# One transfer instead of two halves for the first K block of a cached-attention kernel

## The chip, the cores and the metric

The kernel runs on one core of a Trainium2 chip. The metric is device time in microseconds (us) of one execution. Three runs of the kernel before the change took 1298.83, 1298.94 and 1298.96 us, so the median is 1298.94 us.

A core has a matrix engine (TensorE, "PE" in the rows, with its weight loads as "PEld"), a vector engine (VectorE, "DVE"), a scalar engine (ScalarE, "ACT"), GpSimd ("POOL") and a sync engine (SyncE, "SP") which here only issues DMA transfers. Transfers run on 16 DMA engines. On-chip memory has 128 partitions; a "row" of a transfer below is what one partition receives.

## The reference

The computation is one decoding step: layer norm of x, attention of one query against a long cache, a small MLP as a gate, and a residual. Sizes: 2 batches, 32 heads, 8192 cached keys per head, 128 elements per key, all in 32-bit floats.

```python
def _A_ref(x, k_cache, v_cache, wq, wo):
    q = (x @ wq).reshape(B, Sq, H, Dh).transpose(0, 2, 1, 3)
    scores = jnp.einsum("bhqd,bhkd->bhqk", q, k_cache) * (Dh ** -0.5)
    p = _softmax(scores, axis=-1)
    o = jnp.einsum("bhqk,bhkd->bhqd", p, v_cache)
    return o.transpose(0, 2, 1, 3).reshape(B, Sq, H * Dh) @ wo

def _B_ref(x, w1, b1, w2, b2):
    h = _gelu(jnp.einsum("bsd,df->bsf", _layernorm(x), w1) + b1)
    return jnp.einsum("bsf,fd->bsd", h, w2) + b2

xn = _layernorm(x)
return x + _A_ref(xn, k_cache, v_cache, wq, wo) * _silu(_B_ref(xn, w1, b1, w2, b2))
```

The caches are nearly all of the data: K and V hold 268 MB each.

## The kernel before

The 64 combinations of batch and head are worked off as N = 32 pairs. The K of a pair is a block of 128 partitions by 64 KB (128 keys of 128 floats on each partition, 8.39 MB), and so is its V. There are three such buffers: `kb[0]` and `kb[1]` take the K blocks in turn (pair n goes to `kb[(n+1) % 2]`, so pair 0 goes to `kb[1]`), and `vb` takes the V blocks. Before the pairs, `kb[0]` holds the query weights wq and `vb` the MLP weights and the start's small tensors.

For a pair n the work is:

- `scores_mul` (L555, DVE, once for each half s of the block, 64 keys per partition each): multiply K by the query, in place.
- `scores_sum` (L562, DVE, once for each half): sum over the 128 elements, which gives the scores.
- `max_rows` (L566 on DVE, L569 on PE) and `max_dve` (L572, DVE): the maximum, which crosses partitions by a transpose on PE.
- `exps` (L578 on PE, L579 to L587 on ACT): the exponentials, PZ.
- `weighted` (L606 on PE, 64 matmuls): probabilities times V.
- `spread` (L621, DVE): the result put in its place for the final projection.

The loop over pairs is software-pipelined by hand. While DVE works on the scores of pair n, it also does the maximum of pair n-1, between the two multiplications of pair n, and after it ACT and PE do the exponentials and the weighted sum of pair n-1. Pair 0 and pair 31 stand outside a hardware loop; pairs 1 to 30 are 15 turns of a loop with two pairs in each turn.

All loads are issued by SP, in program order, on one DMA queue, by the helper `load` at L329. The order is: w1, x, w2, b1, b2, wq, K of pair 0, K of pair 1, V of pair 0, K of pair 2, V of pair 1, and so on to K of pair 31, V of pair 30, V of pair 31 (into `kb[1]`), and the pieces of the output weights wo (into `vb`). Below, k0, k1, ... and v0, v1, ... stand for these K and V transfers. SP waits before a load until its buffer is free: k1 for the query matmuls L513 that read wq, v0 for the last reader of the start's tensors, k(n+2) for the scores of pair n (the row is that of L566), v(n) for the matmuls L606 of pair n-1.

Three kinds of blocks come as two transfers of 32 KB a row: K of pair 0, K of pair 31 and V of pair 31. All others are one transfer of 64 KB a row. Each kind of transfer has a semaphore of its own on which its readers wait: the halves of k0 have k10 and k11, the whole blocks of `kb[0]` and `kb[1]` have kb0 and kb1.

A planner (`Plan`) records all operations, works out from the tiles read and written which semaphore values each must wait for, and writes them out in program order; it moves nothing. Inside the hardware loop a wait's value is a multiple of the turn, plus a constant where that is needed; a constant costs a register instruction.

Of the kernel before, what the change touches and what calls it, by code (L numbers as in the profile page):

```python
# [164 lines left out]
def decode_kernel(nc, x, kc, vc, wq, wo, w1, b1, w2, b2, out):  # L165
# [9 lines left out]
    N = B * HH  # L175
# [152 lines left out]
    def load(dst, src, sem, w, over=()):  # L328
        op("sp", lambda: nc.sync.dma_start(dst, src), (), w, over=over, dma=sem)  # L329

    def load_k(n):
        i = (n + 1) % 2
        if n in (0, N - 1):
            for s in range(2):
                load(kbuf[i][:, s * M:(s + 1) * M], kf[n][:, s * M:(s + 1) * M], f"k{i}{s}", [("kb", i, s)])
            return
        load(kbuf[i], kf[n], f"kb{i}", [("kb", i, s) for s in range(2)])
# [10 lines left out]
    for t, src, k in ((b1_sb, b1, "b1"), (b2_sb, b2, "b2")):  # L348
        load(t.rearrange("o (k e) -> o k e", k=16), src.rearrange("(o k e) -> o k e", o=1, k=16), k, [k])
    load(wq_sb, wq.rearrange("(p c) n -> p c n", p=P), "wq", [("kb", 0, s) for s in range(2)])  # L350
    load_k(0)


# [177 lines left out]

    PT, PM, PN = (t for t in scratch[:3])
    load_k(1)

    def load_v(n):
# [90 lines left out]
    for n in range(N):  # L626
        scores_mul(n, 0)
        if n:
            max_dve(n - 1)
            exps(n - 1)  # L630
        scores_mul(n, 1)

        if n:
            weighted(n - 1)
            if n < N - 1:
                load_v(n)
        scores_sum(n, 0)
        scores_sum(n, 1)
        max_rows(n)
        if n:  # L640
            spread(n - 1)

        if n + 2 < N:
            load_k(n + 2)
        elif n + 2 == N:
            for s in range(2):
                load(kbuf[1][:, s * M:(s + 1) * M], vf[N - 1][:, s * M:(s + 1) * M], f"v1{s}", [("kb", 1, s)])
# [104 lines left out]
```

## Time and profile before

The profiled execution took 1298.91 us; its span, from the first to the last instruction, is 1297.6 us, so 1.31 us lie around it. It is 0.03 us below the median of the runs.

| | profile before |
|---|---|
| time of the profiled execution | 1298.91 us |
| span | 1297.6 us |
| DVE busy | 1138.0 us, 88% of the span |
| PE busy | 407.6 us, 31% |
| data moved by DMA | 559.42 MB, 431 GB/s mean |
| first multiplication of pair 0 on DVE starts | 52.27 us |
| last piece of wo used from | 1293.51 us |

In the rows of the profile, a line of a timeline gives start, length, engine, source line, operation, output and input, count, and in brackets the idle time before it with what ended that. A line of a window gives the window, then busy time and count on each engine, the clock granted to TensorE, the DMA engines' busy share and the GB/s that landed in the window. "DMA to landing" is the time from the issue on SP to the transfer's completion, as least, median and greatest of the transfers in the lines above it.

### The profile page before, as it was taken

Reading aid. Unit: us, or ns where it says so; the run is one execution under the profiler, and the core shown is the slowest. Engines: PE = TensorE matmul, PEld = TensorE weight load, DVE = VectorE, ACT = ScalarE, POOL = GpSimd, SP = SyncE. Lnnn points to the kernel's source line nnn. Section 1 sums busy time; section 2 is a strip of 40 time slices with the busy share of each in tenths; the row PEclk is TensorE's granted clock in tenths of the full one; section 3 lists DMA queues with packets and bytes.
Section 4 is the critical chain, followed back from the end, with each engine's and each line's share of the span. In section 5 each row is a group of like instructions: output and inputs, shape, how many; then the busy total and the mean of one; then the engine's idle time right before and its main releaser. Section 6 shows DMA issues by size and latency. Waiting matters only on the chain.

```text
span 1297.6 us, 6944 instructions
## 1 busy us (share of the span) xinstructions
PE 407.6 (31%) x2796; PEld 123.4 (10%) x2796; DVE 1138.0 (88%) x294; ACT 78.0 (6%) x250; POOL 1.4 (0%) x8
## 2 busy tenths in 40 slices
PE   5703333312333312333311333321333321233328
PEld 1100110000101000101100101100001100001103
DVE  3599999988889988889988888988888988888991
ACT  1200000000000000000000000000000000000000
POOL 0000000000000000000000000000000000000000
PEclk9856666556666656666656666656666655666658
DMA  9999999999999999999999999999999999999998
GB/s 404 445 425 440 428 432 438 426 444 424 434 438 424 446 424 440 430 426 444 426 438 430 430 440 426 444 424 434 438 424 446 424 432 438 424 446 426 425 433 372
DMA packets 11231, 559.42 MB, mean 431 GB/s; under 512 B 1364, under 2 KB 1620, under 8 KB 1880
## 3 DMA queue, kind: packets, MB, share of 16 engines
q1 hardware_dynamic: 11224, 559.33, 99.7%
q8 instruction: 4, 0.07, 0.0%
q14 instruction: 3, 0.02, 0.0%
HBM read 559.30 MB, written 0.03 MB: 431 GB/s over the span
## 4 chain that ended last, share of the span: by engine, by line
DMA 71%; PE 24%; DVE 3%; issue 1%; ACT 0%; SPq 0%; DVEq 0%
DMA vb<-in_A_v_cache_dram 68%; PE po L606 22%; DMA vb<-in_A_wo_dram 2%; DVE kb L555 1%; DVE sc L562 1%; PE s L433 1%; DMA vb<-in_A_x_dram 1%; PE po L513 1%; PE s L479 0%; PE s L435 0%; DVE vb L441 0%; DVE vb L380 0%; ACT L454 0%; PE acc L696 0%; PE s L486 0%
## 5 line engine op out<-in xcount | busy, mean ns | idle before, releaser
L555 DVE TENSOR_TENSOR kb<-kb,Q 128x8192 f32<-128x8192 f32 x64 | 555.5, 8681 | 99.6 <-DMA kb<-in_A_k_cache_dram 93.1
L562 DVE TENSOR_REDUCE sc<-kb 128x64 f32<-128x8192 f32 x64 | 552.3, 8666 | 0.0
L606 PE MATMUL po<-vb,PZ 128*8 128x512 f32 x1984 | 282.3, 733 | 286.1 <-DMA vb<-in_A_v_cache_dram 284.8
L578 PE MATMUL s<-nm,srow 1*128 1x2 f32 x64 | 18.6, 358 | 360.8 <-DVE nm L572 360.8
L606 PEld LDWEIGHTS po<-vb,PZ 128*8 128x8 f32 x1984 | 56.3, 103 | 485.9 <-issue 482.4
L569 PE MATMUL s<-ident,mx 128*1 128x128 f32 x32 | 11.8, 369 | 197.8 <-DVE mx L566 197.8
L578 PEld LDWEIGHTS s<-nm,srow 1*128 1x128 f32 x64 | 15.9, 306 | 370.1 <-DVE nm L572 370.1
L613 ACT COPY o<-po 128x512 f32<-128x512 f32 x32 | 18.8, 586 | 528.2 <-PE po L606 528.2
L579 ACT COPY bias<-s 128x2 f32<-128x2 f32 x32 | 5.1, 160 | 623.9 <-PE s L578 623.9
L615 PE MATMUL s<-mod,o 128*128 128x2 f32 x256 | 33.6, 253 | 22.1 <-ACT o L613 22.1
L615 PEld LDWEIGHTS s<-mod,o 128*128 128x128 f32 x256 | 31.1, 191 | 51.4 <-ACT o L613 51.4
L583 ACT ACTIVATE PZ<-sc,bias 64x128 f32<-64x128 f32 x64 | 25.5, 399 | 1.8
L569 PEld LDWEIGHTS s<-ident,mx 128*1 128x1 f32 x32 | 2.5, 79 | 201.4 <-DVE mx L566 170.8
L621 DVE TENSOR_TENSOR Z<-blk,s 128x8 f32 (+1 forms) x32 | 5.2, 163 | 13.3 <-PE s L615 13.3
L441 DVE COPY vb<-vb 2x384 f32<-2x384 f32 x4 | 1.8, 499 | 15.4 <-ACT vb L437 15.4
L433 PE MATMUL s<-vb 128*2 128x512 f32 (+1 forms) x24 | 12.1, 654 | 0.3 <-ACT vb L393 0.3
L583 ACT ACTIVATION_READ_ACCUMULATOR PZ<-sc,bias 64x1 f32 x64 | 11.8, 185 | 0.0
L566 DVE TENSOR_REDUCE mx<-sc 128x1 f32<-128x128 f32 x32 | 9.2, 286 | 1.1
L587 ACT ACTIVATE ZR<-half,rs 128x8 f32 (+1 forms) x32 | 9.6, 301 | 4.1
L606 PE MATMUL po<-kb,PZ 128*8 128x512 f32 x64 | 9.4, 754 | 1.4 <-ACT PZ L583 1.4
L572 DVE TENSOR_REDUCE nm<-s 1x2 f32<-1x128 f32 x32 | 8.7, 272 | 0.3 <-PE s L569 0.3
L688 DVE COPY wide<-x 128x32 f32<-128x32 f32 x1 | 0.2, 195 | 9.0 <-ACT o L686 9.0
(101 smaller groups left out, 90.3 us busy)
## 6 DMA issues: line engine op xcount, KB each, us to landing
kb<-in_A_k_cache_dram SPq DMA_DIRECT2D x4, 4096.0 KB, 42.9
kb<-in_A_v_cache_dram SPq DMA_DIRECT2D x2, 4096.0 KB, 40.9
vb<-in_B_w_dram SPq DMA_DIRECT2D x2, 2752.0 KB, 12.1
vb<-in_A_wo_dram SPq DMA_DIRECT2D x1, 4096.0 KB, 19.0
vb<-in_A_wo_dram SPq DMA_DIRECT2D x1, 2048.0 KB, 23.6
vb<-in_A_wo_dram SPq DMA_DIRECT2D x1, 1280.0 KB, 26.2
vb<-in_A_wo_dram SPq DMA_DIRECT2D x2, 256.0 KB, 26.3
vb<-in_A_v_cache_dram SPq DMA_DIRECT2D x31, 29.5
```

What stands on the lines that cost most here:

```text
L433: pe(lambda f=f, w=w, ph=ph, c=c: matmul(ph[:B, :w], yT[:, c, :], w1_sb[:, c, f:f + w], start=(c == 0), stop=False), ["yT", "w1"], [k])
L513: pe(lambda i=i, c=c, wv=wv, a=a, j=j, hd=hd: matmul(PO[R * j:R * j + NQ * B, :].rearrange("m (h d) -> m h d", d=DH), xnT[:, c, a:a + NQ * ...
L555: vector(n, n, lambda n: nc.vector.tensor_tensor(out=k, in0=k, in1=cols(Q, n * DH, DH).unsqueeze(1).to_broadcast([P, M, DH]), op=ALU.mult) ...
L562: vector(n, n, lambda n: nc.vector.tensor_reduce(out=SC[:, s * M:(s + 1) * M], in_=k, axis=AX.X, op=ALU.add), [("kb", i, s)], [("sc", s)])
L566: vector(n, n, lambda n: nc.vector.tensor_reduce(out=MX, in_=SC, axis=AX.X, op=ALU.max), [("sc", 0), ("sc", 1)], ["mx"])
L569: pe(lambda i: transpose(PM[:1, :P], MX, ident), ["mx", "ident"], ["s1"], it=n, loop=n > 0)
L578: pe(lambda i: matmul(PN[:, :U], srow, NM, start=True, stop=True), ["srow", "nm"], ["s2"], **one)
L583: act(lambda i, r=r, s=s: nc.scalar.activation(PZ[r, :, s, :], sc[r], AF.Exp, bias=BIAS[r, s:s + 1], scale=SCALE, accum_out=RS[r]), ["bias ...
L587: act(lambda i: nc.scalar.activation(cols(ZR, i * UP - UP, UP), half, AF.Copy, scale=RS), ["half"] + [("rs", s) for s in range(U)], [("ZR" ...
L606: pe(lambda i, t=t, j=j, v=v: matmul(PO[R * j:R * j + U * JW, :], PZ[:, t].rearrange("p s j -> p (s j)"), v[:, t * JW:(t + 1) * JW, :].rea ...
L613: act(lambda i: nc.scalar.copy(O4, PO), ["po"], ["o4"], **one)
L615: pe(lambda i, k=k: matmul(PT[:, :U], O4[:, k * DH:(k + 1) * DH], mod[:, k:U * JW:JW], start=(k == 0), stop=(k == JW - 1)), ["o4", "mod"], ...
```

## The change

K of pair 0 is loaded by one transfer of 64 KB a row instead of two of 32 KB a row. K and V of pair 31 stay in halves.

```diff
     def load_k(n):
         i = (n + 1) % 2
-        if n in (0, N - 1):
+        if n == N - 1:
             for s in range(2):
                 load(kbuf[i][:, s * M:(s + 1) * M], kf[n][:, s * M:(s + 1) * M], f"k{i}{s}", [("kb", i, s)])
             return
         load(kbuf[i], kf[n], f"kb{i}", [("kb", i, s) for s in range(2)])
```

On SP's queue, at the start of the program, the difference is the following (in brackets, whom the issue waits for):

```order
 L329 DMA vb<-in_B_b_dram 1x512
 L329 DMA kb<-in_A_wq_dram 128x16384
-L329 DMA kb<-in_A_k_cache_dram 128x8192 x2
+L329 DMA kb<-in_A_k_cache_dram 128x16384
 L329 DMA kb<-in_A_k_cache_dram 128x16384 [waits pe]
 L329 DMA vb<-in_A_v_cache_dram 128x16384 [waits dve]
```

Two issues have become one, at the same place, ahead of the issue of k1 that waits for PE.

On DVE, the end of the start and the scores of pair 0, before the loop:

```order
 L495 TENSOR_TENSOR vb<-vb 128x512
 L498 TENSOR_REDUCE x<-vb 128x32 [waits dve]
-L555 TENSOR_TENSOR kb<-kb,Q 128x8192 [waits act,dma_k10]
-L555 TENSOR_TENSOR kb<-kb,Q 128x8192 [waits dma_k11]
+L555 TENSOR_TENSOR kb<-kb,Q 128x8192 [waits act,dma_kb1]
+L555 TENSOR_TENSOR kb<-kb,Q 128x8192
 L562 TENSOR_REDUCE sc<-kb 128x64 [waits dve] x2
 L566 TENSOR_REDUCE mx<-sc 128x1 [waits dve]
```

The multiplication of the first half now waits for the whole block, on the semaphore kb1; that of the second half has no wait left.

On DVE, inside the loop, ahead of the first multiplication of the even pair of a turn:

```order
 L621 ISA [waits pe]
 L621 TENSOR_TENSOR Z<-blk,s 128x8
+L107 REGISTER_ALU
 L555 ISA [waits dma_kb1]
 L555 TENSOR_TENSOR kb<-kb,Q 128x8192
```

One register instruction per turn has come in, since the first count of kb1 is now taken by k0.

## The prediction

> **What bounds the kernel now.** I read the page first: the busy shares, the DMA lines, and the chain that ended last.
>
> ```profile
> PE 407.6 (31%) x2796; PEld 123.4 (10%) x2796; DVE 1138.0 (88%) x294; ACT 78.0 (6%) x250; POOL 1.4 (0%) x8
> DMA  9999999999999999999999999999999999999998
> q1 hardware_dynamic: 11224, 559.33, 99.7%
> DMA 71%; PE 24%; DVE 3%; issue 1%; ACT 0%; SPq 0%; DVEq 0%
> ```
>
> DVE is busy for 88% of the span, but the one DMA queue is busy for 99.7% of what 16 engines could give, in every slice. DMA is also 71% of the chain. So a microsecond counts only if it makes the queue run dry or move slower. Next come the waits, first of the engines, then of SP's queue.
>
> ```profile
> PE po L606 <- DMA vb<-in_A_v_cache_dram: 284.8, 30, 13.5
> DVE kb L555 <- DMA kb<-in_A_k_cache_dram: 93.1, 26, 3.6
> SPq L329 <- PE po L606: 960.7, 31, 33.1
> SPq L329 <- PE po L513: 45.9, 1, 45.9
> ```
>
> PE waits for V in 30 pairs and DVE for K in 26. SP waits too, for free buffers, but ahead of a queue that still has work. The chain in order of time shows the pace (start, length, what):
>
> ```profile
> 87.30 0.08 DVE kb L555
> ...
> 95.91 0.28 DVE nm L572
> ...
> 98.11 8.88 PE po L606 x64
> 107.01 26.88 DMA vb<-in_A_v_cache_dram
> ...
> 134.01 9.70 PE po L606 x64
> 143.72 28.89 DMA vb<-in_A_v_cache_dram
> ...
> 1188.45 29.11 DMA vb<-in_A_v_cache_dram
> ```
>
> v1 lands at 107.01 + 26.88 = 133.89, v29 at 1217.56. That is 1083.67 us for 28 pairs, 38.70 us a pair and 19.35 us a block of 8.39 MB (433.5 GB/s). From v1 to v29 the queue thus never changes pace, and the question is what happens before v1.
>
> **The start of the queue.** SP's and DVE's timeline, with the landing times of the transfers in question:
>
> ```profile
> 2.56 0.35 SPq L329 DMA_DIRECT2D kb<-in_A_wq_dram  x1
> 49.81 0.33 SPq L329 DMA_DIRECT2D kb<-in_A_k_cache_dram  x1
> 86.78 0.33 SPq L329 DMA_DIRECT2D kb<-in_A_k_cache_dram  x1
> 107.01 0.33 SPq L329 DMA_DIRECT2D vb<-in_A_v_cache_dram  x1
> 122.00 0.33 SPq L329 DMA_DIRECT2D kb<-in_A_k_cache_dram  x1
> 143.72 0.33 SPq L329 DMA_DIRECT2D vb<-in_A_v_cache_dram  x1
> 52.27 17.29 DVE L555 TENSOR_TENSOR kb<-kb,Q 128x8192 f32<-128x8192 f32 x2 [5.90 <-ACT Q L528]
> 122.39 8.69 DVE L555 TENSOR_TENSOR kb<-kb,Q 128x8192 f32<-128x8192 f32 x1
> 157.84 8.69 DVE L555 TENSOR_TENSOR kb<-kb,Q 128x8192 f32<-128x8192 f32 x1 [0.37 <-issue]
> 230.81 8.69 DVE L555 TENSOR_TENSOR kb<-kb,Q 128x8192 f32<-128x8192 f32 x1 [2.80 <-DMA kb<-in_A_k_cache_dram]
> DMA to landing us min/median/max: 33.9/38.6/43.2
> L329 SPq DMA_DIRECT2D kb<-in_A_k_cache_dram x2: 440/456/472, 3.0 to 3.4; - x2
> DMA to landing us min/median/max: 43.2/48.1/52.9
> DMA to landing us min/median/max: 25.9/35.5/45.2
> DMA to landing us min/median/max: 27.8/27.8/27.8
> DMA to landing us min/median/max: 31.2/31.2/31.2
> ```
>
> The landing rows belong, in this order, to wq with the first half of k0; to both halves of k0; to k1 with v0; to k2; to k3. Issue plus landing time gives: wq 2.56 + 33.9 = 36.5, first half of k0 46.2, second half 3.4 + 52.9 = 56.3, k1 49.81 + 25.9 = 75.7, v0 50.2 + 45.2 = 95.4, k2 86.78 + 27.8 = 114.6, k3 122.00 + 31.2 = 153.2. The reader is to see that before the change DVE's first multiplication waits for Q (52.27), six microseconds after its half of K is there, and that the second half, needed at 52.27 plus half of 17.29 = 60.9, lands at 56.3.
>
> **The change part by part.**
>
> *One issue fewer on SP.* Its 0.44 us are covered: SP then waits 45.9 us for L513. Without this cover it would cost or gain 0.44 us. Taken: 0.
>
> *64 KB rows instead of 32 KB rows for 8.39 MB.* The two halves took 56.3 - 36.5 = 19.8 us. The halves of the last pair's K show the price of halves in full flow:
>
> ```profile
> L329 SPq DMA_DIRECT2D kb<-in_A_k_cache_dram x1: 328/328/328, 1194.4 to 1194.4; - x1
> DMA to landing us min/median/max: 42.6/42.6/42.6
> DMA to landing us min/median/max: 15.0/15.0/15.0
> ```
>
> The second of them lands at 1194.4 + 42.6 = 1237.0, 19.4 us after v29 at 1217.56, where both halves are all that came between; a whole block takes 19.35. So halves cost 0.05 us. At the start everything is a little slower, whole rows too: w2, issued at 1.6 and landing after 15.0 (the last row), is in at 16.6, and wq, one transfer with 64 KB a row, then took 36.5 - 16.6 = 19.9 us. Bounds for the change: -0.5 (from 19.8 to a whole block's 19.35) and +0.1 (to wq's 19.9). Nearest is the pair of halves in flow; I take -0.05.
>
> On the price of a transfer the Trainium skill, "DMA: Bandwidth & Descriptors", section "Anatomy of one DMA", fits about 2.0 us plus bytes over 436 GB/s to each DMA on the path issued from GpSimd; by that a transfer fewer would be worth -2.0 us instead of -0.05. The 19.4 us above disagree for transfers queued behind each other: the halves' fixed parts lie under the transfer before.
>
> *DVE waits for the whole block.* The first multiplication starts at k0's landing, 56.3, instead of 52.27: +4.05 us (+3.6 if k0 takes 19.35 us, +4.15 with 19.9). The multiplication of the second half follows without a gap as now, so the whole of DVE's line moves by 4.05. Behind it hang, in this order:
>
> - k2's issue: 86.78 to 90.8, that is 4.6 us before v0 lands (8.6 now).
> - the maximum of pair 0 (95.91), the exponentials and `weighted` (98.11): v1's issue goes from 107.01 to 111.1, which is 3.5 us before k2 lands (7.6 now).
> - k3's issue: 122.00 to 126.1, 7.8 us before v1 lands.
> - v2's issue: DVE's start of pair 2 goes from 122.39 to 126.4. In pair 1 the matmuls L606 followed that start by 10.8 us (98.11 less 87.30), so they start at 137.2 instead of at v1's landing; with 9.7 us, v2 is issued at 146.9 (143.72 now), 6.3 us before k3 lands.
> - pair 3: DVE starts at 161.9 instead of 157.84, L606 at 172.7; v2 lands at 143.72 + 28.89 = 172.6. The delay on V's side is gone.
> - K's side: at 230.81 DVE waited 2.80 us for K; with the delay it comes 1.2 us late there, and the pair after takes up the rest. DVE's pair is 157.84 - 122.39 = 35.4 us long, the queue's 38.70, so 3.3 us of delay go with each pair in which DVE would have waited.
>
> *Does the queue run dry?* The least distance is 3.5 us, at v1. How much it needs I estimate from the windows:
>
> ```profile
> 0.00:2.00 2.00, 0.00 (x0) 0.00 (x0) 0.84 (x12) 1.27 (x1) 1.25 (x8) 1.00 0.58 121
> 0.00:95.40 95.40, 39.70 (x181) 10.34 (x181) 57.59 (x70) 12.47 (x25) 1.42 (x8) 0.78 0.99 424
> 0.00:114.60 114.60, 50.16 (x255) 13.56 (x255) 76.79 (x74) 14.50 (x32) 1.42 (x8) 0.78 0.99 425
> 0.74 0.39 SPq L329 DMA_DIRECT2D vb<-in_B_w_dram  x1
> ```
>
> The first issue is at 0.74 and 242 KB are in by 2.00, so an issue has its engines moving within about 0.9 us. By 114.6, 425 x 114.6 = 48.7 MB had landed; all transfers up to and with k2 are 47.6 MB. The 1.1 MB more are rows of v1 by engines that were done with k2 before the slowest: 2.6 us ahead on average, and up to 1.2 us more for rows under way (a row takes an engine 19.35/8 = 2.4 us). An average engine is free for v1 at 110.8 to 112.0, and v1 would be there at 112.0: it idles 0 to 1.2 us. At k2 it is free at 91.2 to 92.5 (424 x 95.4 = 40.4 MB against 39.2) and the rows are there at 91.7: 0 to 0.5 us. The slowest engine, which lands at 114.6, is busy to near then and idles at neither place, and the end waits for the slowest. Bounds 0 and +1.7 us; I take 0, by the slowest engine.
>
> *A register instruction per turn of the loop.*
>
> ```profile
> L107 DVEq FUSED_REGOPS  x45: 46/53/53, 87.3 to 1170.5; - x45
> ```
>
> 15 x 0.053 = 0.8 us on DVE, each in a pair where DVE has 3.3 us to spare; without that cover +0.8. Taken: 0.
>
> *Sum.* 0 - 0.05 + 0 + 0 + 0: 1298.91 - 0.05 = 1298.9 us, against the runs' median 1298.94.
>
> **The rivals.**
>
> *The queue runs dry in part* (+0.5 to +1.7, about 1300): if the early engines' idling ends up in the slowest one. For it: the distances fall to 4.6 and 3.5 us, less than any the trace shows (6.5 at k1, 56.3 less 49.81). Against it: the slowest has 2.6 us of work left when v1's rows are there.
>
> *The delay goes through to the end* (+4.05, 1303.0): slower. If each later issue hung on DVE, as it would with a queue that is empty whenever SP issues, the 4.05 us would stay. For it: DVE's 88%. It decides once v1's issue comes after k2's landing, which takes 7.6 us of delay at this place; the change brings 4.05. The Trainium skill, "Perfetto Trace Analysis", in its list of remedies, says that splitting a DMA lets some work start sooner where the DMA engines are otherwise idle. Here they are 99.7% busy, so by that condition undoing the split should cost nothing; the earlier start itself, 4.05 us, is real.
>
> *The larger rows pay* (-0.5, 1298.4): if the start's slow 19.8 us came from the halves. For it: k2 to v1 at 19.3. Against it: wq's 19.9 as one transfer.
>
> *Nothing changes on DVE either*: k0 would have to land by 52.3 as one block; at 433.5 GB/s after wq it can't before 55.8.
>
> **How the numbers follow.** Hidden delay 0.60, larger rows pay 0.16, partly dry 0.15, through to the end 0.07, something faster that I don't see 0.02. A difference of 0.2% (2.6 us: under 1296.3 or over 1301.5) is about what a measurement of this kernel can tell from no change. Slower by more: the 0.07 and a third of the partly dry (0.05); faster by more: 0.02 and a little of the larger rows, 0.05 together; the rest, 0.83, within. The range goes from 1298.2 (the -0.5 case with some margin) to 1301.2 (+1.7 with the same), leaving out the delay that goes through.
>
> **What would show it.** In the profile after, DVE's first L555 starts at 56.3, released by DMA instead of Q; k2 and v1 are issued at about 90.8 and 111.1; v1 still lands at 133.9 and the later V's at the same times, 38.70 apart; DVE's waits for K fall from 26 to 25. I am wrong if v1 lands later than 134.5, or if the pair's period changes.

## The result, and the profile after

The changed kernel takes 1300.77 us (median of 22 runs, 1299.61 to 1301.6), the kernel before 1298.88 us (22 runs, 1298.69 to 1298.99). The ratio is 1.0014, with a 95% interval from 1.0008 to 1.002. It is slower, by 1.9 us, which is less than 0.2% but clear of the measurement. The profiled execution after took 1300.19 us, 1.28 us more than the one before; where its trace is read below, these 1.28 us are what has to be found.

The page of the changed kernel, its span, the DMA queue, and the waits of the engines and of SP's queue:

```profile
span 1298.9 us, 6958 instructions
q1 hardware_dynamic: 11080, 559.33, 99.7%
PE po L606 <- DMA vb<-in_A_v_cache_dram: 276.6, 29, 13.5
DVE kb L555 <- DMA kb<-in_A_k_cache_dram: 99.1, 26, 9.2
SPq L329 <- PE po L513: 47.0, 1, 47.0
```

144 packets fewer have moved the same bytes at the same 99.7%. DVE's longest wait for K was 3.6 us and is now 9.2: that is the new one at k0. The number of these waits stays at 26, since another, at 230.81, is gone; the forecast of 25 had left out the new one. PE waits for one V fewer, v1.

SP's and DVE's timeline at the start, and in the last three lines the landing times of wq with k0, of k2, and of v1:

```profile
90.74 0.33 SPq L329 DMA_DIRECT2D kb<-in_A_k_cache_dram  x1
111.13 0.33 SPq L329 DMA_DIRECT2D vb<-in_A_v_cache_dram  x1
125.96 0.33 SPq L329 DMA_DIRECT2D kb<-in_A_k_cache_dram  x1
145.78 0.33 SPq L329 DMA_DIRECT2D vb<-in_A_v_cache_dram  x1
56.23 17.29 DVE L555 TENSOR_TENSOR kb<-kb,Q 128x8192 f32<-128x8192 f32 x2 [9.21 <-DMA kb<-in_A_k_cache_dram]
161.88 8.69 DVE L555 TENSOR_TENSOR kb<-kb,Q 128x8192 f32<-128x8192 f32 x1 [0.37 <-issue]
DMA to landing us min/median/max: 33.9/43.6/53.3
DMA to landing us min/median/max: 24.0/24.0/24.0
DMA to landing us min/median/max: 24.1/24.1/24.1
```

k0, issued at 2.96, lands at 2.96 + 53.3 = 56.3, as its second half did. k2 lands at 90.74 + 24.0 = 114.7 (before: 114.6), and v1 at 111.13 + 24.1 = 135.2 (before: 133.89). From there on nothing changes any more, as the chain shows:

```profile
145.78 28.09 DMA vb<-in_A_v_cache_dram
...
1189.52 29.31 DMA vb<-in_A_v_cache_dram
...
1268.36 26.40 DMA vb<-in_A_wo_dram
```

v2 lands at 173.87 (before: 172.61), v29 at 1218.83 (before: 1217.56), both 1.26 to 1.27 us late; the chain's piece of wo is in at 1294.76 (before: 1293.46), 1.30 us late. The whole difference of this execution has arisen before v1 landed: the block v1 took 135.2 - 114.7 = 20.5 us after k2 instead of a block's 19.35.

The windows around k2's landing show how, the first line before the change, the second after it (the last two columns are the busy share of the DMA engines and GB/s):

```profile
112.00:115.00 3.00, 0.00 (x0) 0.00 (x0) 3.00 (x2) 0.00 (x0) 0.00 (x0) 0.50 1.06 459
112.00:115.00 3.00, 0.83 (x8) 0.74 (x7) 3.00 (x1) 0.00 (x0) 0.00 (x0) 1.00 0.90 328
```

A window counts a row of a transfer whole, bytes and time, where the row begins (the longest dose below shows this). Before, 459 GB/s for 3 us are 21 rows of 64 KB, and 1.06 x 16 x 3 us spread over them is 2.42 us a row. After, only 15 rows begin, so one of the 16 engines still has none of v1, and they take 2.88 us each.

### The profile page after: what moved, and what is told of

Its sections match the earlier page's. It is cut to its first block, busy times and chain, and to the rows that moved or that the text cites. A ratio compares the mean times of both kernels' runs of the same rounds, so it can differ in the third digit from the quotient of the medians.

```text
span 1298.9 us, 6958 instructions
## 1 busy us (share of the span) xinstructions
PE 412.7 (32%) x2796; PEld 124.2 (10%) x2796; DVE 1138.0 (88%) x294; ACT 78.0 (6%) x250; POOL 1.4 (0%) x8
## 3 DMA queue, kind: packets, MB, share of 16 engines
q1 hardware_dynamic: 11080, 559.33, 99.7%
## 4 chain that ended last, share of the span: by engine, by line
DMA 68%; PE 24%; DVE 4%; issue 3%; ACT 0%; another core or an unknown queue 0%; SPq 0%; DVEq 0%
DMA vb<-in_A_v_cache_dram 65%; PE po L606 22%; DMA vb<-in_A_wo_dram 2%; DVE sc L562 2%; DVE kb L555 1%; PE s L433 1%; DMA vb<-in_A_x_dram 1%; PE po L513 1%; PE s L479 0%; PE s L435 0%; DVE vb L441 0%; DVE vb L380 0%; ACT L454 0%; PE acc L696 0%
## 5 line engine op out<-in xcount | busy, mean ns | idle before, releaser
L606 PE MATMUL po<-vb,PZ 128*8 128x512 f32 x1984 | 287.4, 744 | 279.2 <-DMA vb<-in_A_v_cache_dram 276.6
## 6 DMA issues: line engine op xcount, KB each, us to landing
vb<-in_A_wo_dram SPq DMA_DIRECT2D x1, 4096.0 KB, 19.3
```

The lines of the kernel that those rows point to most:

```text
L606: pe(lambda i, t=t, j=j, v=v: matmul(PO[R * j:R * j + U * JW, :], PZ[:, t].rearrange("p s j -> p (s j)"), v[:, t * JW:(t + 1) * JW, :].rea ...
```

## The experiments

Two theories stood against each other at first. "Late issue": the queue needs more notice than I had estimated, so that v1 and perhaps k2 came to it too late. "Larger rows": the 64 KB rows of k0 disturb the queue by themselves. By **notice** I mean how long before the landing of the block ahead of it in the queue a block is issued.

**The wait without the larger rows.** In the kernel before, with k0 in halves, the first multiplication waits for both:

```diff
-            [("kb", i, s)] + qs, [("kb", i, s)])
+            ([("kb", i, 0), ("kb", i, 1)] if n + s == 0 else [("kb", i, s)]) + qs, [("kb", i, s)])
```

> The kernel before, with k0 still in two halves of 32 KB a row; the first multiplication of pair 0 waits for both halves. Nothing is left out of the computation. Theory 'late issue' (the late start of DVE makes k2 and v1 reach the queue too late): DVE starts near 56.3 us, k2 and v1 are issued near 90.8 and 111.1, v1 lands about 1.3 us later than before, and the time is that of the changed kernel, about +1.9 us. Rival 'larger rows' (the 64 KB rows of k0 themselves disturb the queue): the issues are as late, but the time stays at +0.2 us or less. Rival 'through': +4 us.

1300.63 us (11 runs), ratio 1.0015 [1.0006, 1.0024]: 1.75 us slower, like the changed kernel. SP's issues of k2 and v1, and v1's time to landing:

```profile
90.79 0.33 SPq L329 DMA_DIRECT2D kb<-in_A_k_cache_dram  x1
111.26 0.33 SPq L329 DMA_DIRECT2D vb<-in_A_v_cache_dram  x1
DMA to landing us min/median/max: 23.8/23.8/23.8
```

v1 lands at 135.1. The larger rows aren't needed for the loss: the wait alone makes one of the same size.

**Doses of delay on DVE.** In the kernel before, a sum over rows of Q runs on DVE ahead of the first multiplication; its result is overwritten later:

```diff
+    dve(lambda: nc.vector.tensor_reduce(out=SC[:, :15], in_=Q[:, :DH].unsqueeze(1).to_broadcast([P, 15, DH]),
+                                        axis=AX.X, op=ALU.add), [("Q", 0)], [("sc", 0), ("sc", 1)])
     for n in range(N):
         scores_mul(n, 0)
```

With 15, 44 and 66 rows:

> The kernel before, k0 in halves, with a sum over 15 x 128 elements on DVE ahead of the first multiplication (about 2.1 us from 52.3 on). The added sum's result is overwritten and nothing is left out. v1 should be issued near 109.1, 5.5 us before k2 lands. Late issue, with a threshold: the loss of 1.9 us at a delay of 4 us and a slope of one give a threshold near 2 us, so here +0 to +0.3 us. Rival 'each microsecond of delay costs in proportion': +1.0 us.

> As before with a sum over 44 x 128 elements (about 6 us of delay). v1 should be issued near 113.1, 1.5 us before k2 lands, and k2 near 92.8, 2.6 us before v0 lands. Late issue, with a threshold near 2 us and a slope of one: about +3.9 us. The estimate of the prediction (an issue has its rows there within 0.9 us, and the slowest engine decides): +0.3 us. In proportion: +2.9 us.

> As before with a sum over 66 x 128 elements (about 9 us of delay). v1 should be issued near 116.0, after k2 has landed, so every engine is idle. Late issue, threshold near 2 us, slope one: about +7 us. The estimate of the prediction: 116.0 + 0.9 less 114.6 = +2.3 us. In proportion: +4.3 us.

Measured: 1298.87 us (11 runs, three of them at 1300.0 to 1301.8), 1302.74 us (8 runs) and 1304.53 us (5 runs), so -0.0, +3.9 and +5.7 us; the ratios are 1.0005 [0.9996, 1.0014], 1.0028 [1.0018, 1.0039] and 1.0051 [1.0037, 1.0064]. By the medians the first two fit a threshold near 2 us of delay with a slope of one, and the third is a little under it. My estimate of the prediction (+0.3 us for the second dose) is ruled out. A loss in proportion is ruled out only by the third dose: 4.3 us were expected by it, and the interval begins at 4.8, while the first two intervals hold its 1.0 and 2.9 us. The scale of the doses is rough, too: Q was ready at another time in each execution, so v1's issue (108.38, 114.58 and 116.26) came 1.4, 7.6 and 9.3 us later than the 107.01 before.

In the longest dose k2 is issued only after v0 has landed, so its trace shows a block on an idle queue. The issues of v0 and k2 with their times to landing, and then windows around k2's issue:

```profile
49.98 0.44 SPq L329 DMA_DIRECT2D vb<-in_A_v_cache_dram  x1
95.36 0.33 SPq L329 DMA_DIRECT2D kb<-in_A_k_cache_dram  x1
DMA to landing us min/median/max: 45.1/45.1/45.1
DMA to landing us min/median/max: 23.2/23.2/23.2
```

```profile
90.50:92.50 2.00, 0.00 (x0) 0.00 (x0) 2.00 (x1) 0.00 (x0) 0.00 (x0) 0.50 1.21 524
92.50:95.50 3.00, 0.00 (x0) 0.00 (x0) 2.97 (x2) 0.00 (x0) 0.00 (x0) 0.50 0.00 0
95.50:97.50 2.00, 0.37 (x1) 0.08 (x1) 1.77 (x2) 0.00 (x0) 0.00 (x0) 0.50 1.51 524
```

Two things are to be seen. First, on the idle queue k2 takes 23.2 us from issue to landing, 3.85 us more than the 19.35 us of a block in full flow. Second, how the windows count. The 524 GB/s for 2 us are 1.05 MB, 16 rows of 64 KB. A busy share of 1.21 is more than 16 engines can have; spread over the 16 rows it is 2.42 us each, the time that a row takes an engine. So a row is counted whole where it begins: the last rows of v0 begin by 92.5 and end by 94.9, and v0 lands at 49.98 + 45.1 = 95.1. The first 16 rows of k2 begin within 2.1 us of its issue, and by their share of 1.51 they take 3.0 us each instead of 2.42.

About 1.5 of the 3.85 us come from one engine. The trace has a transfer of instructions, 16 KB, that held this engine from 102.09 for 0.95 us; by the trace's records of single rows (start and length of each) it ended its part of k2 at 118.25, the 15 others by 116.8.

**v1 late, k2 on time.** In the kernel before, copies on ACT, which are overwritten later, stand ahead of the first exponentials:

```diff
         if n:
             spread(n - 1)
+        for _ in range(22 if n == 0 else 0):
+            act(lambda: nc.scalar.copy(O4, Q[:, :512]), ["mx"] + [("Q", c) for c in range(512 // (NB * DH))], ["o4"])
```

With 22, 28, 20 and 18 copies:

> The kernel before (k0 in halves, DVE early) with 22 copies on ACT ahead of the first exponentials, so that only the chain to v1's issue is late, by about 4 us; k2 is issued on time near 86.8. Nothing is left out. Theory 'a block issued on an idle queue lands 23.2 us later, 3.85 us over the pace, so an issue needs that much notice before the landing ahead of it': v1 has about 3.6 us of notice, so the loss is 0 to +1.2 us as at v1 in the changed kernel. Rival 'k2's late issue is the cause and v1 only shows it': +0.

> The same with 28 copies: v1 is late by about 8 us, issued near 115, when k2 has landed. By the notice of 3.85 us: v1 lands at 115 + 23.2 = 138.2 instead of 133.9, so about +4.3 us; later V's may still be late by less. Rival 'a late V alone is made good by K': +0 to +1.

> As the runs with copies on ACT, with 20 copies: v1 is issued near 109.8, about 4.7 us before k2 lands, and k2 on time. If 3.85 us of notice are enough: +0 to +0.2 us. If the loss sets in earlier and grows slowly (rows that follow close on their issue are slower): about +0.8 us.

> The same with 18 copies: v1 is issued near 108.5, about 6 us before k2 lands, and k2 on time. By the notice of 3.85 us: +0. The run with 2 us of delay on DVE had the same notice of 6.2 us and was at +0 in most executions but 1 to 3 us slower in three of eleven; if short notice of v1 alone makes these, some executions will be slower here too.

Measured with 22 copies: 1300.89 us (11 runs), ratio 1.0016 [1.0007, 1.0025], 2.05 us over the kernel before. Its issues and the chain at v1:

```profile
86.95 0.33 SPq L329 DMA_DIRECT2D kb<-in_A_k_cache_dram  x1
111.16 0.33 SPq L329 DMA_DIRECT2D vb<-in_A_v_cache_dram  x1
111.16 24.28 DMA vb<-in_A_v_cache_dram
```

k2 is as early as before, DVE is as early as before, k0 is in halves, and only v1 is issued at 111.16: v1 lands at 135.4 and the time is that of the changed kernel. So v1's late issue alone is enough for the whole loss. That is above the 0 to 1.2 us I had expected from 3.85 us of notice.

With 28 copies: 1303.89 us (5 runs), ratio 1.0043 [1.0029, 1.0056], +5.05 us. v1 was issued after k2 had landed and took 21.68 us:

```profile
115.66 21.68 DMA vb<-in_A_v_cache_dram
```

That is 2.3 us over the pace. The overhead of an idle queue is thus no constant: 3.85 us for k2 above, 2.3 us here, where no transfer of instructions falls into the block. v1 lands 3.5 us late; a further 1.25 us of this execution's loss arise only after v30, in the loads of wo.

With 20 copies: 1299.2 us (11 runs, 1298.83 to 1300.97), ratio 1.0006 [0.9997, 1.0015]. With 18 copies: 1298.89 us (11 runs, to 1299.69), ratio 1.0001 [0.9992, 1.0011]. The profiled execution with 18 copies:

```profile
86.83 0.33 SPq L329 DMA_DIRECT2D kb<-in_A_k_cache_dram  x1
109.69 0.33 SPq L329 DMA_DIRECT2D vb<-in_A_v_cache_dram  x1
109.69 24.09 DMA vb<-in_A_v_cache_dram
DMA to landing us min/median/max: 27.6/27.6/27.6
```

k2 lands at 114.4, v1 has 4.7 us of notice and lands at 133.8: no loss. The execution profiled with 20 copies, at 1298.83 us the fastest of its runs, happened to start early and had 5.7 us of notice. Four of its eleven runs took 1300.0 to 1301.0 us; their notice isn't known.

**v1 early, k2 late.** For all pairs the maximum and the exponentials are put ahead of the first multiplication, once in the changed kernel and once in the kernel before:

```diff
-        scores_mul(n, 0)
         if n:
             max_dve(n - 1)
             exps(n - 1)
+        scores_mul(n, 0)
         scores_mul(n, 1)
```

> The changed kernel (k0 in one transfer) with the maximum and the exponentials of the pair before put ahead of the first multiplication on DVE, for all pairs: v1 is issued near 103 instead of 111, k2 still near 90.8. If v1's short notice is the main cause: the time falls back to +0.0 to +0.5 us over the kernel before. If k2's (4.2 us of notice) is: it stays near +1.9 us. If the larger rows are the cause, it stays at +1.9 us too.

> The kernel before with the same order of DVE's work as the last one. All notices are longer than before, none was short: the time stays within 0.3 us of the kernel before. If the queue had hidden waits left elsewhere, it would be faster.

The changed kernel with this order takes 1299.11 us (11 runs, 1298.83 to 1300.48), ratio 1.0005 [0.9996, 1.0014]; the kernel before with it 1298.92 us, ratio 1.0 [0.9991, 1.0009]. Issues and chain of the former:

```profile
90.68 0.33 SPq L329 DMA_DIRECT2D kb<-in_A_k_cache_dram  x1
103.78 0.33 SPq L329 DMA_DIRECT2D vb<-in_A_v_cache_dram  x1
DMA to landing us min/median/max: 24.1/24.1/24.1
103.78 30.31 DMA vb<-in_A_v_cache_dram
```

k2 is as late as in the changed kernel and lands at 114.8 (the third line), k0 is one transfer, but v1 is issued at 103.78 and lands at 134.1, against 133.89 before. At the median 0.27 us of the 1.9 us are left, by the ratio 0.65 us with an interval from -0.5 to +1.8, and five of the eleven runs took 1299.8 us and more. So an early v1 takes back most of the loss at the median; how much of the rest is due to k2's late issue isn't shown. The profiled execution, 1300.06 us, is one of the five, and little of its loss had arisen by v1's landing (see the end of the next section).

All runs together, each worked out from its own issues and landings as above, in us:

| run | k2: notice, then landing after v0 | v1: notice, then landing after k2 | time against before (medians) |
|---|---|---|---|
| before | 8.6, 19.2 | 7.6, 19.3 | 0 |
| before, maximum first | 8.8, 19.3 | 9.1, 19.4 | +0.1 |
| delay of 2 on DVE | 7.6, 19.3 | 6.2, 19.3 | 0.0 |
| 20 copies on ACT | 9.6, 19.4 | 5.7, 19.3 | +0.35 |
| 18 copies on ACT | 8.4, 19.2 | 4.7, 19.4 | 0.0 |
| changed | 4.2, 19.8 | 3.6, 20.5 | +1.9 |
| changed, maximum first | 4.1, 20.0 | 11.0, 19.3 | +0.27 |
| 22 copies on ACT | 8.4, 19.2 | 3.4, 20.9 | +2.05 |
| wait for both halves | 4.1, 19.6 | 3.2, 20.6 | +1.75 |
| delay of 6 on DVE | 1.4, 21.7 | 2.1, 19.9 | +3.9 |
| delay of 9 on DVE | -0.3, 23.5 | 2.3, 20.9 | +5.7 |
| 28 copies on ACT | 8.9, 19.4 | -1.1, 22.8 | +5.05 |

In these executions a block follows at the pace from 4.7 us of notice on; at 4.2 us and less it comes late, at -0.3 us by 4 us. In between the loss doesn't follow the notice alone: v1 was late by 1.5 us at 3.4 and by 0.5 us at 2.1. Since the notice is from single profiled executions and the times are medians, a row's two ends needn't agree, least of all for the runs with a wide spread: with 2 us of delay on DVE three of eleven, with 20 copies four of eleven were over 1 us slower than the kernel before.

## Why the prediction was right or wrong

Right, to a tenth or two: where the delay enters and how it travels. DVE starts at 56.23 (predicted 56.3), k2, v1 and k3 are issued at 90.74, 111.13 and 125.96 (90.8, 111.1, 126.1), pair 3 starts on DVE at 161.88 (161.9). v2 is issued at 145.78, earlier than the predicted 146.9, and V's side is back at the pace from there. The issue saved on SP and the register instruction show in no wait; k0's larger rows neither gain nor lose, which the wait for both halves confirms. For a transfer fewer the prediction had worked out -2.0 us from the fit in the Trainium skill, "DMA: Bandwidth & Descriptors", section "Anatomy of one DMA", which is for DMAs issued from GpSimd; k0 as one transfer, issued from SP, lands at 56.3 as its second half did, so the measurement is against that.

Wrong: the step "Does the queue run dry?", of which I took 0, "by the slowest engine". v1 landed at 135.2, later than the 134.5 that I had named as the sign of being wrong and 1.15 us over the pace behind k2, and the time rose by 1.9 us. Three things in this step don't hold.

- The time of a row. I let every row take an engine 2.4 us once it was there. Rows that begin soon after their issue are slower: 3.0 us for the first rows of k2 in the longest dose, 2.88 us in the changed kernel's window above. The prediction's own line for 0.00 to 2.00 had this: 242 KB are 11 of w1's rows of 22 KB (2.82 MB on 128 partitions), and its share of 0.58 makes 1.7 us for each, where 0.8 us would be in proportion to 2.42 us for 64 KB. That rows begin about 0.9 us after an issue was right: 1.0 us in the longest dose, by the records of single rows.
- The slowest engine. The engine that ends k2 last isn't the one that ends v1 last. By the records of single rows the engines of the changed kernel ended k2 between 112.4 and 114.3, and the first row of v1 began at 112.45. But two engines, done with k2 by 113.3, had their first row of v1 only at 114.35 and 115.38, and these two ended v1 last, at 134.8; k2's slowest ended it at 134.2.
- "2.6 us ahead on average". The 1.1 MB beyond k2 were rows of v1 that had begun, not rows that were through. In the profile before, the engines ended k2 between 112.2 and 114.1, not at 110.8 to 112.0.

The likeliest case should have been the rival "the queue runs dry in part", though slow rows have a larger share in it than idle engines: on the mean of the 16 engines, by the records of single rows, v1 lost 0.7 us in slow rows and 0.3 us in idling. The rival's bounds, 0.5 to 1.7 us, held the profiled execution's 1.28 us but not the median of 1.9. I gave it 0.15, and 0.60 to the hidden delay. Its own reason in the prediction, distances "less than any the trace shows", was the better argument of the two: no row showed that 3.5 us were enough. That the median of 1300.77 lies inside the range up to 1301.2 is due to this rival and its margin, not to the case that I had taken.

The rival "through to the end" fell: 4 us of delay cost 1.9, not 4.05, and the smallest dose cost nothing at the median. Yet the point from which I let it decide, a notice of nothing, was too late: at 4.2 us of notice k2 already lost 0.5 us. The Trainium skill, "Perfetto Trace Analysis", section "DMA Optimizations", names idle DMA engines as the case in which splitting a DMA may help. That undoing a split costs nothing where they are busy was my conclusion from it, and it was wrong: the engines were 99.7% busy, and the wait alone, in effect the undone split, still cost 1.75 us, because the earlier start had given v1 its notice.

What stays open. Why a row that begins soon after its issue is slow, and why single engines have their first row as late as 4 us after the issue (115.38 against 111.13), when in the longest dose all have it within 1.9 us, no run shows. From v30's landing to the chain's piece of wo it took 37.1 to 37.2 us in the profiled executions of the kernel before, of the changed one, of the wait for both halves, of the delay of 9 and of 22 copies, but 38.1 in the changed kernel with the maximum first (which is nearly all of its 1.15 us over the one before, 0.2 us having arisen by v1's landing), 38.0 with the delay of 6 and 38.4 with 28 copies; I didn't follow that. And the runs of the changed kernel spread over 2.0 us, where those before spread over 0.3; that the notice differs from one execution to the next would fit, but it was not measured.

## What to carry to other kernels

A queue that is 99.7% busy still depends on when the next block is issued. Before moving a transfer's release, list the notice of each issue behind it. If a shorter notice than any in the trace comes out, count it as a loss until a run shows otherwise. What a block takes on an idle queue beyond the pace is no safe measure: the trace before gave 2.7 us for it (w1, issued at 0.74, took 9.2 us for 2.82 MB, which is 6.5 us at 433.5 GB/s) and the run with 28 copies 2.3, but 3.6 us of notice lost 1.15 us and 4.2 still 0.5. Here 4.7 us were enough for a block of 8.4 MB in one profiled execution, though kernels with 5.7 and 6.2 us in theirs had slower runs too. A small split at the very start made the difference between 3.6 and 7.6 us for a block issued 50 us later.

## What the runs showed of the hardware that was not expected

A block of 8.39 MB takes 21.7 to 23.2 us from issue to landing on an idle queue and 19.35 us behind another one, while the output's 28 KB are through 1.4 us after their issue. Rows that begin soon after their issue take 2.9 to 3.0 us on average in the two windows shown, instead of 2.42. A transfer of 16 KB of instructions in the middle of a block held one engine, and this one ended 1.5 us after the others. The bytes that the windows count are those of rows that begin, a row's time before they are through. The time at which Q is ready moves between executions: DVE's first work on it started at 52.27 us before, and at 51.08, 53.28 and 51.99 us in the three doses; the kernel before, with 7.6 us of notice at v1, still spreads over only 0.3 us.
